# A Mamba-2 scan fused with a squared-ReLU FFN: the hand-written list of steps rewritten up to the fifth unit

## The chip, the cores and the metric

The kernel runs on one core of a Trainium2 chip. The metric is device time in microseconds (us) of one execution. The core has five engines that each take their instructions strictly in program order: TensorE (PE, with its weight loads shown as PEld), VectorE (DVE), ScalarE (ACT), GpSimd (POOL) and SyncE (SP). They wait for each other and for DMA transfers on semaphores. DMA transfers are issued here from SP, ACT and POOL.

## What is computed

The first part is a chunked state-space scan over 4 batches x 8 heads x 768 positions (head size 32, state size 16); the second is a feed-forward layer (FFN) over the 3072 tokens that come out of it, 256 wide, with 2048 hidden columns. Cut to what matters:

```python
cum = np.cumsum(log(clip(a, 1e-6, 1)), axis=-1)          # per chunk of 32
M   = einsum('bhin,bhjn->bhij', C, B) * exp(cum_i - cum_j) * causal
y   = einsum('bhij,bhjd->bhid', M, x) + einsum('bhin,bhnd->bhid', C, state) * exp(cum)
state = exp(cum_last) * state + sum_j B_j x_j exp(cum_last - cum_j)
...
x = y.transpose(0, 2, 1, 3).reshape(3072, 256)
h = np.maximum(x @ w_in, 0.0)
out = (h * h) @ w_out
```

## The kernel before, in words

**Units.** The work is cut into 12 units of 256 tokens, a batch and a third of the sequence each; units 0 to 3 are the first third of the four batches. A unit takes the scan's steps and then the FFN on its 256 tokens. Two blocks of PE work make up almost all the time: the FFN's first product (L450, eight groups `a0` to `a7` of four matmuls for unit 0, `b0` to `b7` for unit 1, and so on) and its second product (L481, `A0` to `A7`, `B0` to `B7`). Between them ACT applies the ReLU (L459) and DVE squares (L465, `qa0` ...).

**A unit's scan.** B, C and x are loaded (L134). C is multiplied by running products P of `a` and B is copied, both into `jt` (L167, L175/L179); PE transposes `jt` (L205), ACT and DVE copy the result to `bct` (L218, L220); PE makes the scores (L235) in four PSUM banks; each is multiplied by a mask into `mts`, three directly by DVE (L244) and one by way of an ACT copy `sc` (L249) and a product in SBUF (L253). x is divided by P into `xs` (L187). Then PE makes the state update `u` and the product within the chunk (`ina`, `inb`: scores' first and second pair), a carry from the unit's own first half (`ca`, which needs `Sd`, L383), all L260, and the unit's FFN input T is copied out of PSUM in two halves (`t`, L218 or L220).

**P.** `a` comes in two loads: one for units 0 to 3 (64 rows, `a_nat64`) and one for the later thirds (128 rows, `a_nat128`, four transfers `la0` to `la3`). Each is clamped (`ac`, L604), scanned by DVE (`sk`, L533) and spread by small fp32 matmuls (L507 to L517, L594, L620). The second set of fp32 products is the step `p`.

**The order.** The string `ORDER` (L48 to L69) is a list of steps in the order in which they are written down, and the function `one` turns each into instructions. Engines run ahead of each other as far as their semaphores let them, so the list fixes the order on each engine and on each queue, not the times. After a colon stands an engine: `v` DVE, `a` ACT, `p` POOL, `s` the SP queue. `idN:C` is N filler matmuls of C columns (L540). `wi0` to `wi3` and `wo0` to `wo3` load the eight weight pieces (`w_in_b0` ..., L148, L152); they are issued by POOL, in POOL's own order. `ldB3`, `ldC3`, `ldx3` load unit 3's inputs, on SP unless another engine is named. `gB3:v` is a gate: DVE writes one element of unit 3's B buffer (L143), so the load of B into that buffer, and all that stands behind it on SP, starts only after DVE has come to this point of its own order.

**PSUM.** Eight banks: 0 to 5 are handed out by `bank()`, 6 and 7 hold the second product of unit 1 and of the others.

Of the kernel before, what the change touches and what calls it, by code (L numbers as in the profile page):

```python
# [30 lines left out]
def kernel(  # L31
# [16 lines left out]
    ORDER = """  # L48
        fa1:a jz0:v ef jz1:p id3:512 ti fa0:s la0:s id4:512 pi eb ldB0:s ac0:v ldC0:a sk0 ku sp la1:a pbh0:p hd
        id1:256 pc0:v pbl0:v mb:a id2:512 trC0 ps iv:8:16 tcC0:1:a tcC0:0:v trB0 la2:s tcB0:2:v pk id1:512 iv1:0:8  # L50
        id1:512 ldx0:s mt0 wi0 la3:s px0:v ldC1:s ac1:p su id2:512 ldB1:s wi1 ldx1:s u0:67 mk0 fq mk0 mk0 pc1:p sc0
        pb1:a tr1 id2:512 tc1:1:a tc1:0:v jz2:a to ms0:p sf0 sk1 wo0 wi2 px1:p mt1 ina0 inb0 ca0 mk1 mk1 t0:aa sc1 us0
        pp1:a mk1 a0 ldC2:s a1 u1 ina1 ms1:v wo1 wi3 pc2 inb1 p2 pd sf1 ca1 t1:va us1 a3 qa1 ldB2:s qa0 a2 wo2 b0 qa3
        qb0 b1 qb1 fr b2 b3 A0 A1 B0 pb2:p B1 tr2 zb0 qb3 gB3:v ldx2:s ldB3:s ldC3:s ldx3:s b4 a4 iv:32:64 zb1 tc2:1:v
        qa2 tc2:0:v b5 sb1 sb0 qb4 a5 qb2 qa4 mt2 sc2 B3 iv:16:32 px2 pc3 wo3 px3 mk2 mk2 sc2 A3 A2 ms2:v ms2:v qa5 a6
        b6 pb3:a B2 a7 qb5 qa6 b7 u2 ina2 inb2 sf2 ld4 A4 tr3 ca2 tc3:1:v t2:aa B4 us2 B5 tc3:0:v u3:45 pc4 mt3 A5 us3
        sc3 c5 qb7 qb6 mk3 za3 pb4 ldC5:s ldB5:s c3 qa7 c4 qc5 c0 qc3 px4 tr4 ldx5:s pb5 pc5 sa3 c1 c6 ldC6:s tr5
        ldB6:s ldx6:s qc4 qc0 A6 px5 pq A7 wm c2 B6 c7 C0 ms3:v mk3 qc6 mk3 qc7 afC2 pc6 B7 C3 C6 C4 qc1 bk rg4 C1 qc2
        d1 d0 za4 sa4 pb6 mk4 mk4 d3 mk4 C5 d4 qd0 d2 mk4 px6 tr6 ld7 C2 C7 qd1 qd2 qd3 zb3 rg5 sb3 D0 mk5 za5 sa5 D1
        mk5 d5 qd4 D2 pc7 pb7 d6 qd5 d7 qd6 D3 zb2 e0 qd7 mk5 e1 qe0 sb2 D4 mk5 D5 tr7 ld8 e2 qe1 D6 e3 qe2 ml px7 rg6  # L60
        e4 D7 qe3 za6 sa6 zb6 mk6 e5 qe4 sb6 e6 qe5 e7 qe6 iv:64:96 mk6 E0 E1 E2 E3 ldC9:s ldB9:s px8 mk6 f0 qe7 E4 f1
        qf0 pc8 E5 pb8 tr8 ldx9:s E6 mk6 f2 qf1 f3 qf2 E7 rg7 mk7 F0 f4 qf3 za7 F1 F2 f5 qf4 f6 qf5 f7 qf6 g0 qf7 zb7
        sa7 sb7 mk7 F3 mk7 F4 pc9 pb9 tr9 px9 ld10 g1 qg0 F5 mk7 g2 qg1 zb4 sb4 F6 g3 qg2 F7 rg8 za8 zb8 sa8 sb8 g4
        qg3 G0 mk8 g5 qg4 G1 mk8 g6 qg5 G2 g7 qg6 G3 mk8 h0 qg7 G4 pc10 pb10 tr10 px10 ld11 h1 qh0 G5 mk8 zb5 sb5 h2
        qh1 G6 h3 qh2 G7 rg9 za9 zb9 sa9 sb9 h4 qh3 H0 mk9 h5 qh4 H1 mk9 h6 qh5 H2 h7 qh6 H3 mk9 i0 qh7 H4 pc11 pb11
        tr11 px11 i1 qi0 H5 mk9 i2 qi1 H6 i3 qi2 H7 rg10 za10 zb10 sa10 sb10 i4 qi3 I0 mk10 i5 qi4 I1 mk10 i6 qi5 I2
        i7 qi6 I3 mk10 j0 qi7 I4 j1 qj0 I5 mk10 j2 qj1 I6 j3 qj2 I7 rg11 za11 zb11 sa11 sb11 j4 qj3 J0 mk11 j5 qj4 J1
        mk11 j6 qj5 J2 j7 qj6 J3 mk11 k0 qj7 J4 k1 qk0 J5 mk11 k2 qk1 J6 k3 qk2 J7 rg12 k4 qk3 K0 k5 qk4 K1 k6 qk5 K2
        k7 qk6 K3 l0 qk7 K4 l1 ql0 K5 l2 ql1 K6 l3 ql2 K7 l4 ql3 L0 l5 ql4 L1 l6 ql5 L2 l7 ql6 L3 ql7"""  # L69
# [370 lines left out]
    hbs, h2s = {}, {}  # L440

    def mm1(blk, fp, c=None, h=None):

# [4 lines left out]
        for i in range(2):
            for g in range(2):
                nc.tensor.matmul(pp[:, h, i * 256:(i + 1) * 256] if c is None else  # L450
                                 _fap(pp, h * 512 + i * 256 + c * 64, [[128, 2], [1, 64]]),
                                 _fap(w, g * w.shape[2] + (o // 2) * 512 + 2 * (o % 2) + i, [[4, 128]]),
                                 T[blk][:, g].rearrange("p r u t -> p (r u t)") if c is None else T[blk][:, g, :, c],
                                 start=(g == 0), stop=(g == 1), skip_group_check=True)
        return h
# [17 lines left out]
    def mm2(blk, fp, rs=(0, 1), cols=None):  # L473
        h2 = h2s[(blk, fp)]
        gi, o = group_of(WOUT, fp)
        for i in range(2):
            for r in rs:
                first = fp == 0 and i == 0 and (r == 0 or blk == NU - 1)
                for c0, c1 in ((0, 256),) if cols is None and (blk < NU - 1 or r == 0) else cols or ((0, 128), (128, 256)):
                    dst = acc(blk, r) if c1 - c0 == 256 else pp[:, 1 + c0 // 128, 0:128]  # L480
# [392 lines left out]
```

## Time and profile before

| what | value |
|---|---|
| median of three runs (lowest, highest) | 113.99 us (113.51, 115.2) |
| profiled execution, first to last instruction | 112.7 us |
| PE busy | 106.8 us, 95% |
| DVE, ACT, POOL busy | 80.7, 76.7, 50.2 us |
| the eight weight loads, issue to landing | 4.7 to 7.5 us |
| filler matmuls (L540) | 15, 5.9 us, the last before 10.1 us |

The page gives no time of the profiled execution but its span; against the median of the runs it is 1.3 us short, which is what lies before the first and behind the last instruction, and the scatter of the runs. PE's share of busy time is an average: in the first 15 us, where the scan of the first units has to come about, PE is partly idle or on fillers, and afterwards it is not. A row of the timeline has the start, the time from the first start to the last end, the engine, the line and the operation with its tiles, and in brackets the idle time of the engine ahead of it with what ended it.

### The profile page before, as it was taken

Reading aid. Unit: us, or ns where it says so; the run is one execution under the profiler, and the core shown is the slowest. Engines: PE = TensorE matmul, PEld = TensorE weight load, DVE = VectorE, ACT = ScalarE, POOL = GpSimd, SP = SyncE. Lnnn points to the kernel's source line nnn. Section 1 sums busy time; section 2 is a strip of 40 time slices with the busy share of each in tenths; the row PEclk is TensorE's granted clock in tenths of the full one; section 3 lists DMA queues with packets and bytes.
Section 4 is the critical chain, followed back from the end, with each engine's and each line's share of the span. In section 5 each row is a group of like instructions: output and inputs, shape, how many; then the busy total and the mean of one; then the engine's idle time right before and its main releaser. Section 6 shows DMA issues by size and latency. Waiting matters only on the chain.

```text
span 112.7 us, 3678 instructions
## 1 busy us (share of the span) xinstructions
PE 106.8 (95%) x1449; PEld 92.3 (82%) x1450; DVE 80.7 (72%) x188; ACT 76.7 (68%) x158; POOL 50.2 (45%) x96
## 2 busy tenths in 40 slices
PE   7985799999999999999999999999999999999990
PEld 2433699897998989989979989889899899899980
DVE  1697867996793899969966989779588298355440
ACT  1554884986894785685687686777876867867840
POOL 7489961586476654394064792184440020000000
PEclk9999999999999999999999999999999999999999
DMA  1999999799979997979787878698950020020203
GB/s 32 194 191 184 197 210 212 127 178 192 154 137 82 125 268 79 118 192 66 100 160 87 162 152 92 134 145 102 185 126 0 6 96 0 25 68 6 93 0 93
DMA packets 67281, 13.44 MB, mean 119 GB/s; under 512 B 63104, under 2 KB 65984, under 8 KB 67264
## 3 DMA queue, kind: packets, MB, share of 16 engines
q1 hardware_dynamic: 64320, 10.88, 60.1%
q0 software_dynamic: 1664, 2.10, 11.1%
q10 hardware_dynamic: 1280, 0.23, 1.1%
q8 instruction: 11, 0.18, 0.6%
q14 instruction: 6, 0.05, 0.1%
HBM read 10.58 MB, written 3.15 MB: 122 GB/s over the span
## 4 chain that ended last, share of the span: by engine, by line
PE 88%; SPq 3%; DMA 3%; POOL 2%; ACT 1%; issue 1%; ACTq 0%; POOLq 0%
PE pp L450 38%; PE pp L481 38%; PE pp L260 7%; DMA C_nat<-in_C_dram 3%; PE pp L229 2%; PE pp L235 2%; SPq L642 1%; PE pp L205 1%; SPq L134 1%; POOL a_cl L604 1%; POOL w_in_b L148 1%; POOL jt L167 1%; ACT T L218 1%; ACT bct L218 0%; SPq L117 0%
## 5 line engine op out<-in xcount | busy, mean ns | idle before, releaser
L459 ACT ACTIVATE hb<-pp 128x512 bf16<-128x512 f32 x96 | 54.5, 601 | 21.7 <-PE pp L450 21.2
L450 PE MATMUL pp<-T,w_in_b 128*128 128x256 bf16 x384 | 53.4, 273 | 0.6 <-ACT T L218 0.6
L481 PE MATMUL pp<-w_out_b,h 128*128 128x256 bf16 (+1 forms) x400 | 53.8, 268 | 0.0
L465 DVE TENSOR_TENSOR h<-hb 128x512 bf16<-128x512 bf16 x96 | 41.9, 451 | 13.0 <-ACT hb L459 12.5
L450 PEld LDWEIGHTS <-w_in_b 128*128 128x128 bf16 x384 | 41.4, 114 | 2.6 <-issue 1.1
L481 PEld LDWEIGHTS <-h 128*128 128x128 bf16 x400 | 37.6, 98 | 4.5 <-issue 1.0
L244 DVE TENSOR_TENSOR mts<-pp,mask 128x512 bf16<-128x512 f32 x43 | 28.5, 677 | 1.4 <-PE pp L229 0.8
L187 POOL TENSOR_TENSOR xs<-x_nat,Pinv 128x256 bf16<-128x256 f32 (+1 forms) x19 | 13.8, 738 | 14.2 <-PE pp L260 6.9
L371 POOL TENSOR_TENSOR Sd<-z,Pquad 128x256 bf16<-128x256 f32 x16 | 10.6, 672 | 12.9 <-DVE z L355 6.7
L167 POOL TENSOR_TENSOR jt<-C_nat,P_sb 128x128 bf16<-128x128 f32 x22 | 9.4, 447 | 5.5 <-DMA C_nat<-in_C_dram 5.5
L355 DVE SCALAR_TENSOR_TENSOR z<-z,Ptot,us 128x64 f32<-128x64 f32 x8 | 3.6, 446 | 7.7 <-ACT us L339 5.2
L175 POOL CAST jt<-B_nat 128x256 bf16<-128x256 f32 x9 | 4.6, 512 | 5.7 <-DMA B_nat<-in_B_dram 5.7
L488 ACT COPY osb<-pp 128x512 f32<-128x512 f32 x11 | 6.4, 583 | 0.4 <-PE pp L481 0.4
L540 PE MATMUL pp<-const-bfloat16-1.0 128*128 128x512 bf16 (+1 forms) x15 | 5.9, 525 | 0.8 <-PEq L857 0.8
L260 PE MATMUL pp<-mts,xs 64*32 64x128 bf16 (+1 forms) x288 | 5.5, 219 | 0.0
L260 PE MATMUL pp<-bct,Sd 128*128 128x128 bf16 x40 | 4.2, 220 | 0.0
L260 PEld LDWEIGHTS <-xs 64*32 64x32 bf16 (+1 forms) x288 | 3.6, 93 | 0.4 <-issue 0.2
L540 PEld LDWEIGHTS <-const-bfloat16-1.0 128*128 128x128 bf16 x16 | 1.6, 121 | 2.3 <-issue 2.2
L205 PE MATMUL pp<-eye_b,jt 128*128 128x128 bf16 x24 | 2.4, 221 | 1.1 <-POOL jt L167 1.0
L205 PEld LDWEIGHTS <-jt 128*128 128x128 bf16 x24 | 1.7, 100 | 2.1 <-POOL jt L167 1.4
L220 DVE COPY bct<-pp 128x384 bf16<-128x384 bf16 (+1 forms) x7 | 2.3, 336 | 1.5 <-PE pp L205 0.8
L260 PEld LDWEIGHTS <-Sd 128*128 128x128 bf16 x40 | 3.0, 98 | 0.3
(76 smaller groups left out, 60.6 us busy)
## 6 DMA issues: line engine op xcount, KB each, us to landing
out_dram<-osb SPq DMA_DIRECT2D x11, 256.0 KB, 2.9
x_nat<-in_x_dram SPq DMA_DIRECT2D x6, 256.0 KB, 4.2
w_in_b<-in_moe_w_in_dram POOLq DMA_DIRECT2D x4, 256.0 KB, 7.0
w_out_b<-in_moe_w_out_dram POOLq DMA_DIRECT2D x4, 256.0 KB, 6.8
B_nat<-in_B_dram SPq DMA_DIRECT2D x6, 128.0 KB, 3.8
C_nat<-in_C_dram SPq DMA_DIRECT2D x12, 64.0 KB, 3.9
B_nat<-in_B_dram SPq DMA_DIRECT2D x12, 64.0 KB, 3.7
x_nat<-in_x_dram SPq DMA_DIRECT2D x6, 128.0 KB, 3.0
```

The costliest lines, as they stand in the source:

```text
L167: eng.tensor_tensor(out=_fap(jt[k % 3], 128 + 144 * g, [[384, 2], [32, 4], [1, 16]]), in0=_fap(loaded[k]["C"], 128 * g, [[16, 2], [32, 4], ...
L187: eng.tensor_tensor(out=_fap(xs, 256 * r, [[256, 2 // n], [32, 8], [1, 32]]), in0=_fap(loaded[k]["x"], 32 * r, [[32, 2 // n], [64, 8], [1, ...
L205: nc.tensor.transpose(pp[:, h, o:o + 64].bitcast(BF16), jt[k % 3][:, r, w, :], eye_b)
L244: nc.vector.tensor_tensor(out=live[k]["mts"][:, q].rearrange("p r g i -> p (r g i)"), in0=pp[:, q, :], in1=mask1 if k >= LATE else mask, o ...
L260: nc.tensor.matmul(dst, w, v, start=bool(need), stop=False, skip_group_check=True, **({} if pos is None else {"tile_position": pos}))
L371: nc.gpsimd.tensor_tensor(out=_fap(S_d, 0, [[128, 2], [32, 4], [1, 32]]), in0=_fap(z, 0, [[32, 2], [0, 4], [1, 32]]), in1=_fap(Pquad, 4 * ...
L450: nc.tensor.matmul(pp[:, h, i * 256:(i + 1) * 256] if c is None else _fap(pp, h * 512 + i * 256 + c * 64, [[128, 2], [1, 64]]), _fap(w, g ...
L459: nc.scalar.activation(out=hb.rearrange("p i t -> p (i t)"), in_=pp[:, h, :], func=AF.Relu)
L465: nc.vector.tensor_tensor(out=h2, in0=hb, in1=hb, op=ALU.mult)
L481: nc.tensor.matmul(dst, h2[:, i, r * 128:(r + 1) * 128], w_out_b[gi][:, 2 * o + i, c0:c1], start=first, stop=(fp == 7 and i == 1), skip_gr ...
L488: nc.scalar.copy(out=osb, in_=pp[:, 6 if blk == 1 else 7, :])
L540: nc.tensor.matmul(pp[:, h, 0:int(cols)], ones_b[:, 0:128], ones_b[:, 0:int(cols)] if dep is None else dep, start=True, stop=True, skip_gr ...
```

## The change

The list is rewritten up to the fifth unit, `bk rg4`; from there on it reads as before. At the start `tri`, `pick` and `quad` go ahead of the identity `eye_f` on POOL; `wi0` and `wi1` follow right behind `eye_f` and around `eye_b`, ahead of the clamp of `a_nat128`. B of unit 0 is loaded on ACT's queue ahead of C, and x of unit 0 earlier on SP. Unit 0's `xs` moves from DVE to POOL (`px0:p`), a half of its B cast from POOL to ACT. On PE unit 0's `u`, `ina` and `inb` come ahead of unit 1's transposes and scores (before: behind them). The fp32 products `p` come ahead of unit 1's `u` and of the first FFN groups; the scan `sk1` they need stands on DVE behind T of unit 0 (before: ahead of unit 1's masks). The first two FFN groups `a0` and `a1` come behind unit 1's `u` and `ina`. The load of x of unit 2 goes behind the gate `gB3`, and `wo3` goes behind `px3`, `pc4` and `pb4` on POOL.

The code besides the list: `ph_carry`, `mm1` and `mm2` get a second form that cuts a product into four column strips (`strips`, used once the step `cm` has been met), and a few step names that no list used (`x`, `r`, `y`, `w`) go. The new list has no `cm`, so `cols` stays empty and each product is issued as before.

```diff
     ORDER = """
-        fa1:a jz0:v ef jz1:p id3:512 ti fa0:s la0:s id4:512 pi eb ldB0:s ac0:v ldC0:a sk0 ku sp la1:a pbh0:p hd
...
-        pp1:a mk1 a0 ldC2:s a1 u1 ina1 ms1:v wo1 wi3 pc2 inb1 p2 pd sf1 ca1 t1:va us1 a3 qa1 ldB2:s qa0 a2 wo2 b0 qa3
+        id1:256 id3:256 jz0:v la2:s ti pi id4:256 fa0:s fa1:a ac0:v ku jz1:p ef wi0 ldB0:a sk0 la0:s hd eb ldC0:a id3:128 id2:256 la1:a pbl0:v mb:a id1:256 pbh0:a sp ps trB0 id2:256 id2:512 pc0:v wi1 ...
+    cols = []
+
+    def strips(dst, w, v, **flags):
+
+        if not cols:
+            nc.tensor.matmul(dst, w(0, 128), v, skip_group_check=True, **flags)
+            return
+        for c in range(4):
+            nc.tensor.matmul(dst[32 * c:32 * c + 32], w(32 * c, 32), v, skip_group_check=True,
+                             tile_position=(0, 32 * c), **flags)
...
-                nc.tensor.matmul(pp[:, h, i * 256:(i + 1) * 256] if c is None else
-                                 _fap(pp, h * 512 + i * 256 + c * 64, [[128, 2], [1, 64]]),
...
+                strips(pp[:, h, i * 256:(i + 1) * 256], lambda c, n: _fap(w, col + 4 * c, [[4, n]]),
+                       T[blk][:, g].rearrange("p r u t -> p (r u t)"), start=(g == 0), stop=(g == 1))
```

What this does to the engines stands in the built programs' order. The number behind a tile's name is the unit's or the piece's (`xs0` is unit 0's, `w_in_b0` the first piece), the last number only tells buffers apart. Line numbers of the kernel after are lower, by 20 where the list alone shifts them.

POOL near the start, before, from unit 0's share of the B cast to unit 1's `xs`:

```order
L179 CAST jt0_110<-B_nat0_144 128x2x4x16
L148 DMA w_in_b0_113<-in_moe_w_in_dram 128x2x512
L604 TENSOR_SCALAR a_cl128_101<-a_nat128_99 128x128
L148 DMA w_in_b1_114<-in_moe_w_in_dram 128x2x512
L167 TENSOR_TENSOR jt1_111<-C_nat1_207,P_sb_106 128x2x4x16 x2
L253 TENSOR_TENSOR mts0_202<-sc0_3_240,mask_90 128x512
L152 DMA w_out_b0_117<-in_moe_w_out_dram 128x1024
L148 DMA w_in_b2_115<-in_moe_w_in_dram 128x2x512
L187 TENSOR_TENSOR xs1_262<-x_nat1_216,Pinv_107 128x512
```

The same engine and place in the kernel after, from unit 1's cleared `jt` on:

```order
L573 MEMSET jt1_111 128x768
L536 AFFINE_SELECT eye_f_88<-const-float32-1.0 128x128
L128 DMA w_in_b0_113<-in_moe_w_in_dram 128x2x512
L536 AFFINE_SELECT eye_b_89<-const-bfloat16-1.0 128x128
L128 DMA w_in_b1_114<-in_moe_w_in_dram 128x2x512
L596 TENSOR_SCALAR a_cl128_101<-a_nat128_99 128x128
L147 TENSOR_TENSOR jt1_111<-C_nat1_218,P_sb_106 128x2x4x16 x2
L167 TENSOR_TENSOR xs0_233<-x_nat0_183,Pinv_107 128x512
L233 TENSOR_TENSOR mts0_209<-sc0_2_224,mask_90 128x512
L128 DMA w_in_b2_115<-in_moe_w_in_dram 128x2x512
L132 DMA w_out_b0_117<-in_moe_w_out_dram 128x1024
L167 TENSOR_TENSOR xs1_323<-x_nat1_312,Pinv_107 128x512
```

Both identities and both first weight issues now stand ahead of the clamp, and unit 0's `xs` has come in between unit 1's C product and unit 0's last masked score `mts0`.

DVE before, from the copy of unit 1's transposed `bct` to unit 1's T:

```order
L220 COPY bct1_243<-pp_121 128x384
L383 TENSOR_TENSOR Sd0_0_257<-pp_121,Pquad_109 128x256
L533 SCALAR_TENSOR_TENSOR cp128_103<-a_cl128_101,const-float32-0.0 128x128
L244 TENSOR_TENSOR mts1_280<-pp_121,mask_90 128x512 x3
L253 TENSOR_TENSOR mts1_280<-sc1_2_320,mask_90 128x512
L383 TENSOR_TENSOR Sd1_0_403<-pp_121,Pquad_109 128x256
L220 CAST T1_407<-pp_121 128x4x64
```

DVE after, over the same steps:

```order
L200 COPY bct1_285<-pp_121 128x384
L368 TENSOR_TENSOR Sd0_0_316<-pp_121,Pquad_109 128x256
L224 TENSOR_TENSOR mts1_311<-pp_121,mask_90 128x512 x3
L200 CAST T0_331<-pp_121 128x4x64
L525 SCALAR_TENSOR_TENSOR cp128_103<-a_cl128_101,const-float32-0.0 128x128
L602 TENSOR_SCALAR pick_p128_105<-pick_95,cp128_103 128x16
L233 TENSOR_TENSOR mts1_311<-sc1_0_314,mask_90 128x512
L458 TENSOR_TENSOR h20_0_383<-hb0_0_380 128x512
L368 TENSOR_TENSOR Sd1_0_385<-pp_121,Pquad_109 128x256
L200 CAST T1_415<-pp_121 128x4x64 x2
```

The scan `cp128` has moved behind three masks and a half of T of unit 0, and the square of the first FFN group (`h20_0`) has come ahead of unit 1's `Sd1`.

POOL before, from unit 2's `xs` to unit 3's:

```order
L187 TENSOR_TENSOR xs2_563<-x_nat2_491,Pinv_107 128x512
L167 TENSOR_TENSOR jt0_110<-C_nat3_494,P_sb_106 128x2x4x16 x2
L152 DMA w_out_b3_120<-in_moe_w_out_dram 128x1024
L187 TENSOR_TENSOR xs3_568<-x_nat3_496,Pinv_107 128x512
L167 TENSOR_TENSOR jt1_111<-C_nat4_669,P_sb_106 128x2x4x16 x2
```

POOL after, from there to the last weight issue:

```order
L167 TENSOR_TENSOR xs2_519<-x_nat2_508,Pinv_107 128x512
L356 TENSOR_TENSOR Sd0_1_521<-z0_1_505,Pquad_109 128x256
L167 TENSOR_TENSOR xs3_573<-x_nat3_553,Pinv_107 128x512
L356 TENSOR_TENSOR Sd1_1_603<-z1_1_516,Pquad_109 128x256
L147 TENSOR_TENSOR jt1_111<-C_nat4_577,P_sb_106 128x2x4x16 x2
L155 CAST jt1_111<-B_nat4_579 128x2x2x4x16
L132 DMA w_out_b3_120<-in_moe_w_out_dram 128x1024
```

The issue of `w_out_b3` has moved behind unit 3's `xs` and unit 4's C product and B cast. The SP queue after, around the gate, which the load of `B_nat3` waits for, reads:

```order
L114 DMA C_nat3_475<-in_C_dram 128x8x32
L114 DMA B_nat3_457<-in_B_dram 128x8x32
L114 DMA x_nat2_508<-in_x_dram 128x8x64
L114 DMA x_nat3_553<-in_x_dram 128x8x64
L114 DMA C_nat4_577<-in_C_dram 128x8x32
L114 DMA B_nat4_579<-in_B_dram 128x8x32
```

Unit 2's x, which before stood ahead of `B_nat3`, is now behind it, and C of unit 3 is ahead.

More of the change, by code (lines that the diff above doesn't have):

```diff
@@ L54 @@
[L54 to L58, printed above, removed]
@@ L471, in acc, with mm2 @@
         return pp[:, 6 if blk == 1 else 7, r * 256:(r + 1) * 256]
-    def mm2(blk, fp, rs=(0, 1), cols=None):
+    def mm2(blk, fp, rs=(0, 1), parts=None):
         h2 = h2s[(blk, fp)]
@@ L478, in mm2 @@
                 first = fp == 0 and i == 0 and (r == 0 or blk == NU - 1)
[L479 to L483 removed]
+                for c0, c1 in ((0, 256),) if parts is None and (blk < NU - 1 or r == 0) else parts or ((0, 128), (128, 256)):
+                    strips(acc(blk, r) if c1 - c0 == 256 else pp[:, 1 + c0 // 128, 0:128],
+                           lambda c, n: h2[:, i, r * 128 + c:r * 128 + c + n], w_out_b[gi][:, 2 * o + i, c0:c1],
+                           start=first, stop=(fp == 7 and i == 1))
     def ph_out(blk):
@@ L740, in late_banks @@
             busy.difference_update(turn)
-        ups = {}
         def dep(name):
```

48 lines of the change are left out of this document (12 added, 36 removed).

## The prediction, on record before the kernel after was run

> **What bounds the kernel now.** I read the page first (span, engines, chain), then the busy time by stages, then the chain in order of time around the rewritten part, then the timeline of the engines that feed it.
>
> ```profile
> span 112.7 us, 3678 instructions
> ...
> PE 88%; SPq 3%; DMA 3%; POOL 2%; ACT 1%; issue 1%; ACTq 0%; POOLq 0%
> ```
>
> The chain is 88% PE. Whether PE can lose or win anything depends on the stage, so the next view is PE's busy time by stage (columns: stretch, its length, PE, PEld, DVE, ACT, POOL busy, clock, DMA share, GB/s).
>
> ```profile
> 7.90:12.07 4.17, 2.12 (x63) 1.26 (x60) 3.54 (x8) 1.98 (x6) 4.13 (x7) 1.00 1.23 190
> 12.07:14.70 2.63, 2.63 (x75) 2.18 (x76) 2.16 (x6) 1.95 (x7) 2.62 (x5) 1.00 1.14 212
> 14.70:35.70 21.00, 21.00 (x281) 18.88 (x279) 16.39 (x43) 16.19 (x37) 11.32 (x20) 1.00 1.09 166
> 35.70:110.00 74.30, 74.01 (x978) 67.01 (x976) 54.33 (x120) 52.75 (x103) 26.91 (x49) 1.00 0.60 98
> ```
>
> From 12.07 us on PE has no idle time that a new order could remove: 21.00 of 21.00, 74.01 of 74.30. So the time is the moment at which PE becomes dense, plus a fixed amount of work, plus each new wait. The chain shows what PE still owed at the start and its pace (start, length, what).
>
> ```profile
> 12.07 1.05 PE pp L450 x8
> 13.12 0.73 PE pp L260 x48
> 13.85 0.35 PE pp L507 x8
> 14.20 0.21 PE pp L511 x4
> ...
> 14.70 2.69 PE pp L450 x24
> 17.40 1.75 PE pp L481 x16
> 19.14 0.34 PE pp L205 x6
> ...
> 21.23 0.35 PE pp L235 x16
> ```
>
> A group of four FFN matmuls takes 0.44 us (1.75/4) in either product. By 14.70 PE has done `a0`, `a1`, unit 1's scan products, the fp32 products and unit 1's carry `ca1`. The kernel after must do the same set, so I compare when it has done it.
>
> **First term: the front.** The edits that decide are on POOL and DVE.
>
> ```profile
> 0.90 0.29 POOL L544 TENSOR_SCALAR_AFFINE_SELECT eye_f<-const-float32-1.0 128x128 f32<-128x128 f32 x1 [0.40 <-POOLq L857]
> ...
> 3.94 0.19 POOL L544 TENSOR_SCALAR_AFFINE_SELECT quad<-quad 128x4 f32<-128x4 f32 x1
> ...
> 5.98 0.93 POOL L148 DMA_DIRECT2D w_in_b<-in_moe_w_in_dram  x1 [0.25 <-issue]
> ...
> 6.99 0.80 POOL L604 TENSOR_SCALAR a_cl<-a_nat 128x128 f32<-128x128 f32 x1
> ...
> 7.85 0.78 POOL L148 DMA_DIRECT2D w_in_b<-in_moe_w_in_dram  x1
> ...
> 8.66 0.77 POOL L167 TENSOR_TENSOR jt<-C_nat,P_sb 128x128 bf16<-128x128 f32 x2
> ...
> 9.38 1.14 POOL L253 TENSOR_TENSOR mts<-sc,mask 128x512 bf16<-128x512 bf16 x1
> ...
> 11.79 1.07 POOL L187 TENSOR_TENSOR xs<-x_nat,Pinv 128x512 bf16<-128x512 f32 x1
> ```
>
> From 0.90 to 4.13 POOL before made `eye_f`, the cleared `jt`, `tri`, `pick`, `eye_b` and `quad`. After, it makes the same ahead of `w_in_b0`, without `eye_b` (about 0.25, an identity like `eye_f`): `eye_f`, now last, is done at 3.9. Then `w_in_b0` is issued (0.25 + 0.93, to 5.0), `eye_b` 0.25, `w_in_b1` 0.8 (6.1), the clamp 0.86 (7.0; its last `a` had landed by 6.99 before, and stands one place further ahead on SP now), unit 1's C 0.75 (7.8), unit 0's `xs` 1.05 (8.9), `mts0` 1.14: **10.0 us**. PE waits there: the second half of unit 0's `inb` needs `mts0`, and in the new order unit 1's transposes and scores stand behind it. That B of unit 0 is on ACT's queue ahead of C, and `eye_f` late, I cost at nothing: the wait for `mts0` covers both. Unit 0's scores have until about 7.5, since two direct masks (1.85 for three, a row below) and `u` then still end ahead of 10.0; only a C that landed 2 us late would take over from there.
>
> ```profile
> 9.91 0.48 ACT L218 COPY bct<-pp 128x384 bf16<-128x384 bf16 x1 [2.05 <-PE pp L205]
> ...
> 10.42 0.87 DVE L533 TENSOR_TENSOR_SCAN cp<-a_cl,const-float32-0.0 128x128 f32<-128x128 f32 x1
> ...
> 11.21 1.85 DVE L244 TENSOR_TENSOR mts<-pp,mask 128x512 bf16<-128x512 f32 x3
> ...
> 12.74 1.10 ACT L459 ACTIVATE hb<-pp 128x512 bf16<-128x512 f32 x2
> ...
> 13.87 0.42 DVE L383 TENSOR_TENSOR Sd<-pp,Pquad 128x256 bf16<-128x256 f32 x1 [0.47 <-PE pp L260]
> ...
> 14.21 0.41 DVE L220 CAST T<-pp 128x256 bf16<-128x256 f32 x1
> ...
> 14.54 0.96 DVE L465 TENSOR_TENSOR h<-hb 128x512 bf16<-128x512 bf16 x2
> ```
>
> From 10.0: rest of `inb` 0.2, six transposes 0.34 and some 0.2 to their end (10.75), the ACT copy 0.5 (11.3), scores from 11.3. DVE gets its first mask 0.5 later and does three in 1.85 (13.65), then its half of T 0.41 (14.05; ACT's half lies beside the masks), and only **then** the scan 0.87 (14.9). Before, the scan lay in DVE's gap from 10.42 while PE made the scores, free of charge. Now it is behind the masks, and PE waits for it, for `p` stands ahead of unit 1's `u` and of `a0`. That is the wait the change adds, and all of PE's work is queued behind it. Then `p` 0.35 + 0.21 + 0.1 (15.6), `u` and `ina` 0.5 (two thirds of the 0.73 for 48; 16.1), `a0` 0.44 (16.5). The carry `ca1` needs `Sd1`, which on DVE stands behind the square of `a0`: ReLU 0.6 with some 0.15 of latency (17.25), square 0.45 (17.7), `Sd1` 0.42 (18.1), carry 0.2; `inb` and `a1` fit in meanwhile. So the set is done at 18.3 instead of 14.70: **+3.6 us**. T comes first in the new order, yet about 2 us later than before, when `a0` began at 12.07.
>
> **Second term: the last weight piece.** Before, `w_out_b3` was issued at 24.55, with unit 2's x loaded long before the gate.
>
> ```profile
> 18.80 0.37 SPq L134 DMA_DIRECT2D B_nat<-in_B_dram  x1
> ...
> 19.42 1.36 POOL L371 TENSOR_TENSOR Sd<-z,Pquad 128x256 bf16<-128x256 f32 x2 [3.59 <-DVE z L360]
> ...
> 24.55 0.61 POOL L152 DMA_DIRECT2D w_out_b<-in_moe_w_out_dram  x1
> ...
> 26.90 0.39 POOL L175 CAST jt<-B_nat 128x256 bf16<-128x256 f32 x1
> ```
>
> The times to landing, in the order of the sentence behind them (DMA issues: tile, queue, count, KB each, median us to landing):
>
> ```profile
> DMA to landing us min/median/max: 4.7/4.7/4.7
> ...
> w_out_b<-in_moe_w_out_dram POOLq DMA_DIRECT2D x4, 256.0 KB, 6.8
> ...
> x_nat<-in_x_dram SPq DMA_DIRECT2D x6, 256.0 KB, 4.2
> ...
> x_nat<-in_x_dram SPq DMA_DIRECT2D x1, 256.0 KB, 3.5
> ...
> w_in_b<-in_moe_w_in_dram POOLq DMA_DIRECT2D x1, 256.0 KB, 5.7
> ```
>
> The 4.7 is that of the issue at 24.55 and 6.8 the median of the four; 4.2 is the median of six loads of x and 3.5 the shortest in this part, that of unit 0; 5.7 is that of `w_in_b0`, issued at 5.98. After, POOL must do `xs2`, `Sd0`, `xs3`, `Sd1`, unit 4's C and its B cast before the issue, and `xs2` waits for an x that SP issues only behind the gate. Counted from the gate G: the load of B is issued at G+0.1 and takes SP 0.4, x of unit 2 follows at G+0.5 and lands 4.2 us later, G+4.7. POOL then works 1.06 + 0.68 + 1.06 + 0.68 + 0.77 + 0.39 = 4.6: issue at G+9.3, landing at G+14.0. PE needs the piece (`A6`) after its own work since `b0`: G comes about 1.35 behind `b0` (ACT has three ReLUs queued at 0.5, then a square), and from `b0` to `A6` stand 20 FFN groups x 0.44, two sets of transposes 0.7, scores 0.35, unit 2's products and carry 0.7: 10.5. So `A6` is due at G+9.2 and waits **4.8 us**. Nothing hides it, PE is in order. At the low end x lands after 3.5 us and the wait is 4.1; at the high end the piece takes the 6.8 of the median: 6.9. I take 4.8, since loads of inputs run beside it as at 24.55, when it took 4.7.
>
> **What costs nothing.** `strips`, `mm1`, `mm2`, `ph_carry`: the same instructions. Fillers: those before were done by 10.1 and those after end ahead of 10.0, so the wait for `mts0` covers both; if that cover went, those behind the scores, seven of 128 columns, would cost at most 0.8 (0.45/4 each, by the row of the fillers below). Weights earlier: `w_in_b0` would land near 10 (4.1 + 5.7), with its first user at 16.1, so nothing is won. The later transposed loads and unit 4's inputs come later too, but PE is then 8 us later.
>
> Sum: 3.6 + 4.8 = 8.4 us. The profiled execution, 112.7 us, would become 121.1; the median of the runs stands 1.3 above it, so **122.4 us**, 7.4% slower.
>
> **Rivals.**
>
> - *The piece is not late* (chance 0.14). If x of unit 2 and the piece land in 3 us each, or PE is held elsewhere first, the second term shrinks to under 1 and the time is 117 to 118.5 (113.99 + 3.6 and what is left). For it: at the gate all other weights have landed in the new order. Against: it needs issue by G+4.4, before x has landed.
> - *Dearer by the clock or by queues* (0.2). With the piece at 6.8 us and PE's pace lost: 124.5. PE's pace is visible in its fillers: seven of 512 columns took 3.15 us at the start, two took 0.60 later.
>
> ```profile
> 0.83 3.15 PE L540 MATMUL pp<-const-bfloat16-1.0 128*128 128x512 bf16 x7 [0.83 <-PEq L857]
> ...
> 5.91 0.60 PE L540 MATMUL pp<-const-bfloat16-1.0 128*128 128x512 bf16 x2
> ```
>
> That is 0.45 each against some 0.21 net. If PE fell back to the slow pace in the sparse stretch from 11.7 to 15, the first 3.4 us of FFN would do half their work: +1.7, and 124.1 in all. The Trainium skill (TensorE: Matmul & The Clock Gate, Part 1: The HAM clock gate) says that PE starts at half rate, is released by about 3.4 us of activity, and falls back after an idle window as long; by that rule a fall is possible but not due, for my longest pause is 2.1 us. The trace agrees as far as it goes: sparse use from 7.90 to 12.07 us (2.12 of 4.17) left the eight matmuls at 12.07 at 0.13 each with their latency, the full pace.
> - *Not slower: loads set the pace* (0.07). DMA runs at 212 GB/s around 12 to 14.7, so perhaps the weights were what `a0` and all later work followed; issued 2 us earlier, they would give 112.0. For it: `w_in_b0` issued at 5.98 landed 5.7 later, 0.4 before its first use. Against: that use waited for T, and T comes later now. It decides only if T of unit 0 and the scan are there before 12.0, thus if `mts0` ends before 7.
>
> **Chances and range.** My sum 0.52 (119.5 to 123.5); piece not late 0.14 (117 to 118.5); dearer 0.2 (123.5 to 126); not slower 0.07; the rest 0.07 lies between 114.5 and 117. The range 117 to 125.5 leaves out the last two and the upper end of *dearer*, some 2 in 10. Faster or slower by 2% is about what a measurement of this kernel can tell: slower 0.88, within 0.09, faster 0.03.
>
> **What would show it.** Right: `mts0` on POOL ending near 10, PE idle before the L499 products until the scan, near 15; `A6` waiting for the DMA of `w_out_b` some 5 us, in the thirties; after that a dense PE. Wrong: a first FFN matmul before 14; no PE wait on `w_out_b`; PE idle in later stages.

## The result, and the profile after

The kernel after takes 132.87 us (median of 6 runs, 131.92 to 134.49), the kernel before beside it 114.13 (6 runs, 113.36 to 116.68): a ratio of 1.166, 95% interval 1.158 to 1.174. Slower was forecast, but by 8.4 us, to 122.4; it is 18.7, outside the range. (Here and below, ratios leave disturbed executions out; medians hold all.) The profiled execution spans 131.5 us. Two lines of its page, the span and the shares of the chain that ended last:

```profile
span 131.5 us, 3690 instructions
...
PE 79%; DMA 5%; DVE 5%; ACT 5%; SPq 2%; issue 2%; ACTq 0%; DVEq 0%
```

PE's share of the chain has fallen from 88 to 79%, and DMA, DVE and ACT have 5% each: PE waits for all three. The busy times of the engines, on the page of before and then of after, say how the 18.8 us of span divide:

```profile
PE 106.8 (95%) x1449; PEld 92.3 (82%) x1450; DVE 80.7 (72%) x188; ACT 76.7 (68%) x158; POOL 50.2 (45%) x96
```

```profile
PE 114.5 (87%) x1459; PEld 98.1 (75%) x1459; DVE 84.4 (64%) x191; ACT 77.4 (59%) x157; POOL 50.2 (38%) x94
```

PE's idle time (span less busy time) grew from 5.9 to 17.0 us, by 11.1. Its busy time grew by 7.7 for the same products and a few other fillers: PE not only waits more, it also takes longer over its work. (This is an account, not a price: a faster PE would in part only wait longer.) Where? First the late stage, in the windows of after and then of before (stretch, length, PE, PEld, DVE, ACT, POOL busy, clock, DMA share, GB/s):

```profile
55.00:130.00 75.00, 73.55 (x943) 66.59 (x928) 54.99 (x120) 52.85 (x103) 24.45 (x43) 1.00 0.53 92
```

```profile
36.20:111.20 75.00, 73.51 (x940) 66.58 (x928) 54.33 (x120) 52.80 (x103) 26.41 (x48) 1.00 0.61 100
```

The same 75 us of work: nothing is lost from the sixth unit on, and all 18.8 us of span lie in front of it. The waits of PE in the kernel after (what waited, what for, total us, times, longest):

```profile
PE pp L431 <- DVE mts L224: 3.1, 1, 3.1
PE pp L586 <- ACT pick_p L577: 2.5, 1, 2.5
PE pp L240 <- DVE Sd L368: 2.0, 2, 1.5
PE pp L499 <- DVE cp L525: 1.5, 1, 1.5
PE pp L431 <- ACT sc L229: 1.3, 1, 1.3
```

Of these five the prediction had one, the scan (`cp`). The DMA of `w_out_b`, its second term, is not among them. The rows do not add up to 18.8 either, since a good part of the loss is longer work. The chain in order of time up to unit 2's transposes shows more:

```profile
3.73 7.19 DMA B_nat<-in_B_dram
...
11.00 0.41 ACT jt L155
...
11.60 0.21 ACT pick_p L577
...
11.86 0.59 PE pp L586 x2
...
17.53 0.37 DVE cp L525
...
17.94 0.61 PE pp L499 x8
...
19.75 0.99 PE pp L431 x4
...
21.39 0.42 DVE h L458
21.82 0.35 DVE Sd L368
...
22.20 0.62 PE pp L240 x12
22.82 0.98 PE pp L431 x4
23.80 0.21 PE pp L240 x2
24.01 5.77 PE pp L431 x40
29.78 0.35 PE pp L185 x6
```

Three things are to be seen. Unit 1's B takes 7.19 us to land; ACT's copy of it stands ahead of `pick_p`, and the fp32 matmuls that read `pick_p` (L586) wait for it to 11.86. PE also waits between the two FFN groups `a0` and `a1` (19.75 and 22.82), for a `Sd`. And four FFN matmuls take 0.99 us (19.75), where the kernel before has 0.44: PE runs at half pace, 213 ns from start to start where it was 109, and only from 26.6 us on at the full one. The carry `ca1` is done at 24.01, 9.3 us late (forecast: 3.6).

For the rest a ruler of two marks, the ends of the transposes of units 2 and 3 on PE, serves for all runs (us; "rest" is from the second mark to the end of the span):

| kernel | unit 2 | unit 3 | between | rest |
|---|---|---|---|---|
| before | 19.48 | 26.63 | 7.2 | 86.0 |
| after | 30.11 | 43.08 | 13.0 | 88.4 |

So the loss has three parts: 10.6 us up to unit 2's transposes, 5.8 between those and unit 3's, 2.4 behind them. (By the two lists, the first stretch holds the same 12 FFN groups; the second holds 13 before, and 12 and unit 2's carry after, so that 0.4 us of the last part is only a group that comes later.) In the last part stands one wait that before does not have, for unit 3's `sc`:

```profile
49.11 1.03 PE L431 MATMUL pp<-T,w_in_b 128*128 128x256 bf16 x8 [1.32 <-ACT sc L229]
```

In the second part stands the longest wait, 3.06 us at 33.1. DVE, then POOL, then PE around it (timeline of after: start, first start to last end, engine, operation, idle time ahead):

```profile
32.09 0.42 DVE L458 TENSOR_TENSOR h<-hb 128x512 bf16<-128x512 bf16 x1 [0.95 <-ACT hb L452]
33.24 0.50 DVE L458 TENSOR_TENSOR h<-hb 128x512 bf16<-128x512 bf16 x1 [0.72 <-ACT hb L452]
33.66 0.68 DVE L224 TENSOR_TENSOR mts<-pp,mask 128x512 bf16<-128x512 f32 x1
34.26 1.23 DVE L458 TENSOR_TENSOR h<-hb 128x512 bf16<-128x512 bf16 x1
35.42 0.68 DVE L224 TENSOR_TENSOR mts<-pp,mask 128x512 bf16<-128x512 f32 x1
```

```profile
33.42 0.78 POOL L356 TENSOR_TENSOR Sd<-z,Pquad 128x256 bf16<-128x256 f32 x1
34.17 1.04 POOL L167 TENSOR_TENSOR xs<-x_nat,Pinv 128x512 bf16<-128x512 f32 x1
35.17 0.79 POOL L356 TENSOR_TENSOR Sd<-z,Pquad 128x256 bf16<-128x256 f32 x1
...
37.35 0.59 POOL L132 DMA_DIRECT2D w_out_b<-in_moe_w_out_dram  x1
```

```profile
36.15 1.96 PE L431 MATMUL pp<-T,w_in_b 128*128 128x256 bf16 x12 [3.06 <-DVE mts L224]
...
44.20 0.60 PE L431 MATMUL pp<-w_out_b,h 128*128 128x256 bf16 x4
```

`a6` (36.15) needs a PSUM bank that unit 2's second mask frees. That mask stands behind a square that takes 1.23 us beside POOL's `xs3`; the square at 32.09, nearly by itself, takes 0.42. After the pause PE does eight matmuls at 109 ns and then falls to 213 until 43.7 us. The last row is `A6`, the user of the last weight piece: issued at 37.35, as late as forecast, it lands 4.8 us later, at 42.2, but PE itself comes only at 44.20 and does not wait. Two windows of after give the granted clock of the two slow stretches:

```profile
20.00:26.50 6.50, 5.02 (x39) 3.31 (x38) 2.13 (x6) 2.02 (x5) 0.00 (x0) 1.00 0.37 61
...
36.50:43.50 7.00, 6.47 (x82) 4.68 (x80) 3.47 (x10) 2.75 (x6) 1.84 (x4) 0.53 1.05 159
```

The record shows the second one (0.53) and not the first (1.00): here the pace has to be read from the matmuls' starts.

### The profile page after: what moved, and what is told of

It reads as the page before. It is cut to its first block, busy times and chain, and to the rows that moved or that the text cites. A ratio compares the mean times of both kernels' runs of the same rounds, so it can differ in the third digit from the quotient of the medians.

```text
span 131.5 us, 3690 instructions
## 1 busy us (share of the span) xinstructions
PE 114.5 (87%) x1459; PEld 98.1 (75%) x1459; DVE 84.4 (64%) x191; ACT 77.4 (59%) x157; POOL 50.2 (38%) x94
## 3 DMA queue, kind: packets, MB, share of 16 engines
q0 software_dynamic: 1664, 2.10, 10.6%
## 4 chain that ended last, share of the span: by engine, by line
PE 79%; DMA 5%; DVE 5%; ACT 5%; SPq 2%; issue 2%; ACTq 0%; DVEq 0%
PE pp L431 66%; PE pp L240 7%; DMA B_nat<-in_B_dram 5%; ACT hb L452 2%; DVE mts L224 2%; DVE h L458 2%; PE pp L209 2%; PE pp L215 1%; PE pp L185 1%; SPq L634 1%; ACT sc L229 1%; ACT bct L198 1%; SPq L114 1%; DVE Sd L368 1%; PE pp L499 0%
## 5 line engine op out<-in xcount | busy, mean ns | idle before, releaser
L431 PE MATMUL pp<-T,w_in_b 128*128 128x256 bf16 x384 | 56.4, 281 | 4.4 <-DVE mts L224 3.1
L458 DVE TENSOR_TENSOR h<-hb 128x512 bf16<-128x512 bf16 x96 | 45.1, 482 | 21.1 <-ACT hb L452 20.8
L431 PE MATMUL pp<-w_out_b,h 128*128 128x256 bf16 (+1 forms) x400 | 56.5, 276 | 0.0
L431 PEld LDWEIGHTS <-h 128*128 128x128 bf16 x400 | 38.7, 100 | 4.9 <-issue 0.8
L240 PE MATMUL pp<-mts,xs 64*32 64x128 bf16 (+1 forms) x288 | 6.5, 248 | 2.0 <-DVE Sd L368 2.0
L340 DVE SCALAR_TENSOR_TENSOR z<-z,Ptot,us 128x64 f32<-128x64 f32 x8 | 2.5, 307 | 6.7 <-ACT us L324 5.0
L532 PE MATMUL pp<-const-bfloat16-1.0 128*128 128x256 bf16 (+2 forms) x25 | 5.2, 392 | 0.8 <-PEq L836 0.8
L229 ACT CAST sc<-pp 128x512 bf16<-128x512 f32 x5 | 2.9, 591 | 3.3 <-PE pp L215 3.3
L532 PEld LDWEIGHTS <-const-bfloat16-1.0 128*128 128x128 bf16 x25 | 3.0, 144 | 1.9 <-issue 1.2
L215 PE MATMUL pp<-bct 32*64 32x256 bf16 x96 | 3.1, 324 | 1.1 <-DVE bct L200 0.6
```

The lines of the kernel that those rows point to most:

```text
L215: nc.tensor.matmul(pp[64 * u:64 * u + 64, q, r * 256:r * 256 + 256], bct[32 * q:32 * q + 32, r, 0, u * 64:u * 64 + 64], _fap(bct[32 * q:32 ...
L240: nc.tensor.matmul(dst, w, v, start=bool(need), stop=False, skip_group_check=True, **({} if pos is None else {"tile_position": pos}))
L431: nc.tensor.matmul(dst, w(0, 128), v, skip_group_check=True, **flags)
L458: nc.vector.tensor_tensor(out=h2, in0=hb, in1=hb, op=ALU.mult)
L532: nc.tensor.matmul(pp[:, h, 0:int(cols)], ones_b[:, 0:128], ones_b[:, 0:int(cols)] if dep is None else dep, start=True, stop=True, skip_gr ...
```

## The experiments

My theory after this: the front loses by unit 1's late B, the order on DVE and the half pace, the middle by the uncovered wait for unit 2's masks and what follows. The rival is that the waits are interchangeable: with one gone, the next engine's lateness takes its place. Each edit is to the list; times are medians, ratios are to the kernel before, with 95% intervals. The kernel before had 114.05 beside e1 to e4, 114.46 beside e5 to e8, 113.68 beside e9 to e12, 114.10 beside e13 to e16, and 114.02 beside e17 and e18.

**e1, weights later** (after). The edit:

```diff
- ef wi0 ldB0:a ... pc0:v wi1 iv:8:16 ... ms0:p ina0 inb0
+ ef ldB0:a ... pc0:v iv:8:16 ... ms0:p wi0 wi1 ina0 inb0
```

> The kernel after, but wi0 and wi1 are issued by POOL behind mts0 of unit 0 instead of around eye_b. Theory D (the early weight transfers hold back unit 1's B, which landed 7.2 us after its issue in the kernel after and 3.0 in the one before): B of unit 1 lands within about 4 us of its issue, the wait of PE for pick_p (2.5 us) goes, POOL's chain to mts0 ends about 1.7 us earlier, and the time falls by 2 to 3 us, to about 130. Rival (B of unit 1 was late for another reason, and the front is bound by POOL and DVE as predicted): B stays late, time within 1 us of the kernel after.

130.19 us, 1.144 (1.138 to 1.151): 2.7 us less. B of unit 1 now lands 3.7 us after its issue, and `pick_p` is made at 9.08 in its chain, where it was 11.60:

```profile
9.08 0.21 ACT pick_p L577
```

**e2, more fillers** (after). Wider filler groups in front and new ones behind unit 0's scores, `ca0`, `qa0` and `mt2`:

```diff
- mb:a id1:256 pbh0:a ... mk0 mk0 id5:128 ... sc0 id2:128 ... ca0 t0:av ... qa0 sf1 ... mt2 mk2
+ mb:a id4:256 pbh0:a ... mk0 mk0 id5:512 ... sc0 id3:512 ... ca0 id4:512 t0:av ... qa0 id4:512 sf1 ... mt2 id8:512 mk2
```

> The kernel after with more and wider filler matmuls on PE in its waits: before the first fp32 products, behind unit 0's scores, ahead of the second fp32 products, behind a0, and eight of 512 columns behind unit 2's scores. Theory C (PE runs at half pace to 26.5 us and again from 36.7 to 43.5 because it was too idle before): PE is at full pace (109 ns per 256 columns) by about 10 us and stays there through 45 us, and the time falls by 4 to 7 us, to 126 to 129. Rival (the pace is not what costs, the waits are, and PE is idle there anyway): within 1.5 us of the kernel after, 131.5 to 134.

129.68, single runs from 127.48 to 131.5, too scattered for a ratio. In the profiled execution the full pace comes at about 22.6 us instead of 26.6 and holds behind unit 2's scores. That is 3 us less by the median, 1.4 to 5.4 by single runs: the pace is worth something, but these runs do not say how much.

**e3, weights first** (before, with only this part of the change):

```diff
- id4:512 pi eb ldB0:s ... mt0 wi0 la3:s ... ldB1:s wi1 ldx1:s
+ id4:512 wi0 pi eb wi1 ldB0:s ... mt0 la3:s ... ldB1:s ldx1:s
```

> The kernel before with one part of the change: wi0 and wi1 are issued first on POOL, wi0 behind tri and wi1 behind eye_b, all else as it was. Theory D: unit 1's B or C lands some us later, unit 1's transposes wait for it, and the time rises by 1.5 to 4 us, to 115.5 to 118. Rival (two early weight loads are harmless or a gain, since a0 waited for w_in_b0 nearly as long as for T): 113 to 114.5.

117.76, 1.033 (1.028 to 1.038): 3.7 us slower. In its chain and its PE waits:

```profile
4.37 6.30 DMA B_nat<-in_B_dram
```

```profile
PE pp L205 <- ACT jt L175: 2.9, 1, 2.9
```

Early weight pieces hold back the small input loads, in either kernel: that is shown from both sides.

**e4, no wide fillers in front** (before): `id3:512` and `id4:512` taken out.

> The kernel before without its first seven filler matmuls of 512 columns; no other instruction changes. Theory C: PE stays at half pace (213 ns per 256 columns) well past 12 us, the FFN's first matmuls run at it, and the time rises by 2 to 6 us, to 116 to 120. Rival (pace does not depend on those fillers, or costs nothing): 113.5 to 114.5.

114.54 (10 runs, one of them at 121.26), ratio 1.001 (0.997 to 1.005). Missed: the kernel before reaches its full pace, by 11 us, without these fillers.

**e5, cover behind unit 2's scores** (after):

```diff
- qb5 A2 a5 b4 B3 qb4 ldx3:s mt2 mk2 px3:p qb2 ld4 mk2 ... a7 b6 A3 u2
+ qb5 a5 b4 qb4 ldx3:s mt2 A2 B3 A3 mk2 px3:p ld4 mk2 qb2 ... a7 b6 u2
```

> The kernel after with one place of the list changed: behind unit 2's scores come A2, B3 and A3 (instead of a6 at once), and DVE makes both direct masks of unit 2 ahead of the square it had between them. Theory M (PE waited 3.1 us for a PSUM bank that DVE's masks had to free, since no work of the second product stood behind the scores, and the pause also dropped PE to half pace from 36.7 to 43.5): the wait shrinks to 1 us or less, the pace stays at 109 ns, the time falls by 4 to 7 us, to 126 to 129. Rival P (the prediction's: the last weight piece is what PE waits for in this part): the wait only moves to w_out_b, landing at about 42, and the time falls by under 1.5 us.

132.13, 1.159 (1.150 to 1.168): no gain. The waits of this run show why, the masks' down from 3.1 to 0.9, the one for `Sd` up from 2.0 to 3.8:

```profile
PE pp L240 <- DVE Sd L368: 3.8, 2, 2.4
...
PE pp L431 <- DVE mts L224: 0.9, 1, 0.9
```

**e6, DVE's front** (after): the scan ahead of unit 1's masks, `Sd1` ahead of the square of `a0`.

```diff
- sc1 sf0 wi2 ... t0:av sk1 pp1:v p2 ... ms1:v qa0 sf1 inb1
+ sc1 sf0 sk1 pp1:v wi2 ... t0:av p2 ... ms1:v sf1 qa0 inb1
```

> The kernel after with two steps of DVE's order in the front undone: the scan of the second a and its pick stand ahead of unit 1's masks again, and unit 1's Sd ahead of the square of a0. By the prediction's first term the scan costs 1.5 us and Sd behind ReLU and square another 1 to 1.5: the time falls by 2 to 3 us, to 130 to 131. Rival (PE's pace and the late B of unit 1 set the front, and the gain is taken back): under 1 us.

128.02, 1.123 (1.115 to 1.132): 4.9 less, more than the waits taken away (1.5 for the scan, 1.4 for `Sd`). In its trace the matmuls also reach 109 ns at 21.5 us instead of 26.6, so the edit took away part of the half pace too.

**e7, last piece early** (after): unit 2's x ahead of the gate, `wo3` ahead of `xs2`.

```diff
- gB3:v ... iv:16:32 ldx2:s a4 ... px2:p ... wo3 b7
+ ldx2:s gB3:v ... iv:16:32 a4 ... wo3 px2:p ... b7
```

> The kernel after with the prediction's second term undone: x of unit 2 is issued on SP ahead of the gate again, and wo3 on POOL ahead of xs2. Prediction's theory P (the last piece is waited for): 3 to 5 us faster, 128 to 130. Theory M (the piece landed at 42.2, ahead of its use at about 44, since PE was held elsewhere): within 1 us of the kernel after.

131.95, 1.153 (1.142 to 1.165), 0.9 less, with an interval that overlaps that of the kernel after: as theory M says, the second term of the prediction costs next to nothing in this kernel.

**e8: e1, e5 and e6 together** (after).

> Weights behind mts0, DVE's front order as before and the cover behind unit 2's scores, all three in one kernel. If the causes are separate, the gains add: 2.7 (measured for the weights alone) + 2 to 3 + 4 to 7, giving 120 to 124, and what is left is POOL's longer chain and PE's half pace in the front. If one of them covers another, 125 or more.

128.11, 1.124 (1.116 to 1.132): as e6 alone. `ca1` is done at 18.28, but PE then waits 2.9 us for `w_out_b0`, whose issue now stands behind three pieces of `w_in`, and 2.4 for a `Sd`. The rival is right here.

**e9, Sd behind the products** (after):

```diff
- ms1:v qa0 sf1 inb1 a1 ca1 ... u2 sf2 ina2 inb2
+ ms1:v qa0 inb1 a1 sf1 ca1 ... u2 ina2 inb2 sf2
```

> The kernel after with unit 1's `Sd1` behind `inb1` and `a1`, and unit 2's second `Sd` behind `ina2 inb2`, as the kernel before has them; nothing else. Theory S (PE stands still because the list takes the bank that `Sd` still reads for the product behind it): the two waits for DVE's `Sd`, 1.48 and 0.53 us in the kernel after, go, and the time falls by 1.5 to 2.5 us, to about 131. Rival (the wait only moves on to the next late product of DVE, as it did with unit 2's masks): within 1 us of 132.9.

129.67, 1.140 (1.137 to 1.143): 3.2 less, with the waits for `Sd` gone, 2.0 in all. The place of these two steps is a real part of the loss. Here too the full pace comes earlier, at 23.5 us, so the 3.2 is not the waits alone.

**e10 and e11, the list cut at `ca1`.** e10 has before's list up to `ca1` and after's behind it, e11 the reverse; steps that the first part has or lacks are taken out or put in behind the cut.

> The list of the kernel before up to unit 1's carry `ca1`, and from there on that of the kernel after. Theory A (the two halves of the loss are separate: 9.3 us up to `ca1`, 9.5 behind it): 121.5 to 125, with the waits for unit 2's masks (3 us) and unit 3's scores still there. Rival H (most of the loss behind `ca1` is the half pace that PE brings along from the front): below 119.

> The list of the kernel after up to unit 1's carry `ca1`, and from there on that of the kernel before. Theory A: the 9.3 us of the front, and up to 1.5 more for the half pace that outlasts it: 123 to 125.5. Rival H: the half pace goes on and the work behind `ca1` loses several us here too: 127 or more.

e10: 123.50, 1.087 (1.084 to 1.090), as theory A says of the time; but PE's longest wait there is 3.8 us for unit 2's `Sd`, and none for its masks, so the wait has moved. e11: 129.64, single runs 127 to 133, 1.121 (1.115 to 1.126), more than the 123 to 125.5 of theory A and in the range of rival H. The halves overlap: 9.9 us for one, by the ratio 13.7 for the other, 18.7 for both.

**e12, e10 with cover and Sd** (e5's edit and `sf2` behind `ina2 inb2`).

> As the run with the front of the kernel before, and besides three second-product groups of unit 0 (`A2 B3 A3`) behind unit 2's scores, both of its direct masks ahead of one square, and unit 2's second `Sd` behind `ina2 inb2`. Theory A with these causes (masks 3.1 us, `Sd` up to 2.4, the half pace behind the pause about 3): some 7 us less than the run with the front alone, 115 to 118. Rival (the gain is taken back by the next wait, as when this cover was put into the kernel after): less than 3 us below it.

125.50, scattered (123.25 to 127.15) and without a ratio, no gain to be seen: the rival again. So I tried the suspects by themselves in the kernel before.

**e13, no cover** and **e14, Sd first** (before):

```diff
- qb4 a5 qb2 qa4 mt2 sc2 B3 ... mk2 mk2 sc2 A3 A2 ms2:v ... b7 u2
+ qb4 A2 a5 B3 qb2 qa4 mt2 sc2 ... mk2 mk2 sc2 ms2:v ... b7 A3 u2
```

```diff
- pc2 inb1 p2 pd sf1 ca1 ... u2 ina2 inb2 sf2
+ pc2 sf1 inb1 p2 pd ca1 ... u2 sf2 ina2 inb2
```

> The kernel before with one part of the change alone: the second-product groups `A2 B3` ahead of unit 2's scores and `A3` behind `b6`, as the kernel after has them, so that `a6` follows the scores directly. Theory M (the missing cover is a loss by itself: PE waits for the bank that unit 2's masks free, and the pause brings the half pace): 3 to 6 us slower, with a PE wait on DVE's masks at about 22 us. Rival L (in the kernel before DVE is early enough that only the cover's own 1.3 us, or less, are lost): under 1.5 us.

> The kernel before with another part alone: `Sd1` ahead of `inb1`, and unit 2's second `Sd` ahead of `ina2 inb2`, as the kernel after has them. Theory S (PE must not write the bank that `Sd` still reads, and so stands still until DVE is through): 1.5 to 3.5 us slower, with a PE wait on DVE's `Sd`. Rival (DVE is early enough there): under 0.7 us.

e13: 114.72, 1.007 (1.003 to 1.011): theory M misses, and rival L holds. e14: 116.98, in two groups, five runs from 114.73 to 115.55, whose ratio is 1.011 (1.007 to 1.014), and five from 118.41 to 120.67. By the ratio it costs 1.2 us, under theory S and over its rival; PE does wait for `Sd`, 1.7 us in all. So in the kernel before these edits cost about one per cent or less, against 3.2 us that e9 gave in the kernel after. I read this as DVE being late there; no run tests that by itself.

**e15, front mended** (after: e2's fillers without the one behind `qa0`; e6; `sf2` behind `inb2`; `wi0` behind `ms0:p`, then `wo0`, `wi1`, `wi2`).

> The kernel after with the causes found in its front undone together: `wi0`, `wi1` behind unit 0's masked scores and `wo0` ahead of `wi1` and `wi2`; the scan ahead of unit 1's masks; `Sd1` ahead of the square of `a0`, unit 2's second `Sd` behind `ina2 inb2`; and fillers as in the run with fillers, without the one behind `qa0`. Unit 2's scores stay as they are. Theory A (the causes add up, as long as no new one comes): `ca1` done 3 us later than before or less, the masks' wait of 3 us and the half pace behind it left: 120 to 123.5. Rival (gains are taken back by the next late step, as when three were undone): 126 or more.

128.42, 1.125 (1.115 to 1.134): missed by 5 us, although unit 2's transposes end 5.2 us earlier than in the kernel after. Its PE waits and the wait on its timeline:

```profile
PE pp L430 <- DMA w_out_b<-in_moe_w_out_dram: 2.6, 1, 2.6
```

```profile
38.35 0.60 PE L430 MATMUL pp<-w_out_b,h 128*128 128x256 bf16 x4 [2.57 <-DMA w_out_b<-in_moe_w_out_dram]
```

The prediction's second term is here: `A6` waits for the last piece as soon as PE comes early enough for it. In the kernel after other losses cover it.

**e16, xs2 early** (e10 with x of unit 2 ahead of the gate and `iv:16:32` behind `pb2`).

> As the run with the front of the kernel before (123.5), with x of unit 2 loaded ahead of the gate and its reciprocal taken right behind `pb2`, so that POOL makes `xs2` some 4 us earlier and no longer as the first of a block of six operations beside DVE's squares and masks. Theory Q (behind `ca1` the loss is DVE's: a square takes 0.43 us alone and up to 1.26 beside POOL's products, and DVE is busy all of 25 to 30 us): the squares at 24.8 and 26.0, of 0.67 and 1.23 us, become shorter, the wait of 3.8 us for `Sd` falls by a like amount, and the time by 1 to 2.5 us, to 121 to 122.5. Rival (only the order of DVE's steps counts): within 0.5 us of 123.5.

123.40, 1.071 (1.061 to 1.080), against 123.50 and 1.087 (1.084 to 1.090) of e10. The medians are alike, but the ratio of e16 is that of four runs from 122.09 to 123.83 (the other two: 123.94 and 125.56), and the two intervals do not meet: by the ratios it gains 1.9 us, as theory Q says; by the medians of the runs behind the ratios it is 0.9. `xs2` moved from 23.9 to 21.8 and the wait for `Sd` fell from 3.8 to 3.0. The square at 24.8 took 1.07, though, now beside `xs3` (0.67 in e10), and the next one 0.59 (1.23 in e10), so that shorter squares are only a part of the gain.

**e17 and e18, the list cut at unit 2's scores.** e18 is the kernel before but for the stretch from `ca1` to these scores, which is after's; e17 has after's list up to the scores (with e15's edits except fillers and `sf2`) and before's from there.

> The kernel after with its front mended without fillers (`wi0` behind unit 0's masked scores, `wo0` ahead of `wi1` and `wi2`, the scan ahead of unit 1's masks, `Sd1` ahead of the square of `a0`), and from unit 2's scores on the list of the kernel before. Theory M (the loss behind `ca1` lies in the list from unit 2's scores to the fifth unit, and the causes named for the front carry most of the 9.3 us there): `ca1` done about 4 us later than before, some 2 us of half pace besides: 118 to 121.5. Rival N (the stretch from `ca1` to unit 2's scores, with x of unit 2 behind the gate and `xs2` late, carries it): 124 or more.

> The kernel before except for the stretch from `ca1` to unit 2's scores, which is that of the kernel after (without `A2 B3`, which stay behind the scores). Theory M: 114.5 to 117.5, with the wait of up to 1.8 us for `w_out_b0` left, since `A0` stands directly behind `ca1` there. Rival N: 120 or more, with PE waits on DVE's `Sd` or masks near 27 us as in the run with the front of the kernel before.

e17: 125.23, 1.096 (1.088 to 1.104). e18: 121.23, 1.062 (1.055 to 1.068). Rival N holds: that one stretch alone costs 7 us in the kernel before, 1.4 of it a wait of PE for `w_out_b0`, since `A0` stands directly behind `ca1` there. The ruler for these runs:

| kernel | unit 2 | unit 3 | between | rest |
|---|---|---|---|---|
| e10: before to `ca1`, then after | 20.70 | 33.49 | 12.8 | 88.4 |
| e11: after to `ca1`, then before | 32.21 | 39.36 | 7.2 | 90.4 |
| e18: after only from `ca1` to the scores | 20.94 | 32.98 | 12.0 | 86.3 |
| e17: after, mended, to the scores, then before | 23.58 | 34.66 | 11.1 | 87.6 |

(The profiled execution of e11 was one of its longer ones, so its first mark and its last column are not used.) The 5 us between the marks go with the stretch of list from `ca1` to unit 2's scores, whatever stands in front: 12 to 13 with after's, 11.1 with the mended front, 7.2 with before's. The 2.4 in the rest go mostly with the list behind the scores: present in e10, and with it the wait for unit 3's `sc`, both gone in e18. But e17, which has before's list there, still has 1.6 of it and waits 1.1 us for a `Sd` instead. DVE and PE of the kernel before and of e18, measured from the end of unit 2's transposes (19.48 and 20.94):

```profile
20.58 1.15 DVE L465 TENSOR_TENSOR h<-hb 128x512 bf16<-128x512 bf16 x3
...
21.92 1.22 DVE L244 TENSOR_TENSOR mts<-pp,mask 128x512 bf16<-128x512 f32 x2
```

```profile
24.06 2.36 DVE L457 TENSOR_TENSOR h<-hb 128x512 bf16<-128x512 bf16 x3 [0.72 <-ACT hb L451]
26.35 1.27 DVE L223 TENSOR_TENSOR mts<-pp,mask 128x512 bf16<-128x512 f32 x2
```

```profile
27.68 1.23 PE L430 MATMUL pp<-T,w_in_b 128*128 128x256 bf16 x8 [2.42 <-DVE mts L223]
```

Before, three squares (`qb4`, `qb2`, `qa4`, the same in both lists) began 1.1 us behind the transposes, took 1.15, and the masks began at 2.4. In e18 they begin at 3.1: `qb4` is the first of them on DVE, and its group `b4` is the last of PE's four behind the transposes (before: the first), with ACT copying half of `bct` (`tc2:0:a`) ahead of the ReLUs. They take 2.36, beside POOL's `xs2` (24.14 to 25.39); the masks begin at 5.4. PE has run out of other work and waits, and then runs a dozen matmuls at 213 ns. How much of it is `b4`'s place, how much the stretched squares and how much the pace is not settled: e16, which moved `xs2`, gained 1 to 2 us on e10, the pace was not changed by itself, and `b4` was not moved alone.

## Why the prediction was wrong, step by step

- *POOL's chain to `mts0`* (10.0): right, it ended at 10.41. But PE did not wait for it: `pick_p` held PE to 11.86.
- *"Weights earlier: nothing is won"*: this step failed. I asked what the pieces' users gain, not whom the pieces delay. Measured: 2.7 us (e1), and 3.7 put into the kernel before (e3).
- *PE waits for the scan behind the masks*: right in kind, 1.5 us; e6 took it away.
- *"`inb` and `a1` fit in meanwhile"*: failed. The product within the chunk goes into the bank that `Sd` reads, so PE stood for 1.48 us; e9 gave 3.2 for this and the like place in unit 2.
- *PE's pace*: I held the slow pace for a rival of +1.7 us. It came, to 26.6 us and again from 37.0 to 43.7, and PE's busy time grew by 7.7 us. Its price in time is not separately measured; e2 gives 1.4 to 5.4 us. What brings it in the front stays open too: e2 shortened it with fillers, but e4 took fillers out of the kernel before and it did not come. (The 124.5 given there for a late piece and a lost pace together is that of the late piece alone: 2.1 and 1.7 more than 122.4 are 126.2.)
- *The front, 3.6 us*: measured 9.3 to `ca1`, done at 24.01 instead of 18.3. In the trace 3.3 us of the difference of 5.7 were lost by unit 1's scores already (begun at 14.58 instead of 11.3), 0.7 more by the end of `Sd1` (22.15 instead of 18.1), and 1.7 behind it: I had only the carry there, and PE did `inb`, `a1` and the carry. With most of the front's causes undone (e17) unit 2's transposes are 4.1 us late instead of 10.6; that this is near the 3.6 is chance, since e17 has also lost the wait for the scan from which the 3.6 was made up.
- *The last piece, 4.8 us*: the issue is late as I said (37.35), but PE is later. Zero in the kernel after (e7: 0.9), 2.6 in e15: true of the list, hidden in this kernel. So more than half of the 8.4 us was a wait that did not come.
- *From `b0` to `A6` PE only does its own work, 10.5 us*: this failed most. `b0` began at 26.4 and `A6` at 44.20, 17.8 us. I summed PE's matmuls and never asked whether DVE would have the masks ready: 3.6 us are the waits for a mask (3.06) and for `Sd` (0.53), and most of the rest is the half pace behind the pause, some 3 us by estimate (6.5 us of busy PE from 36.5 to 43.5 at a clock of 0.53). The list between `ca1` and unit 2's scores carries about 5 us (4.8 in e18, 5.6 in e10), the list behind the scores most of the last 2.4.

Direction and some causes were right, the direction by the front alone. The sum was short because it followed one engine between the places I looked at. Two of the signs of being wrong that I had named were there: no wait of PE for `w_out_b`, and PE idle in a later stage.
